# First two channel products of batch 0 in column halves, batch 1's casts and turns and batch 2's first turns in a new order, batch 3 loaded by SP

## The chip, the cores and the metric

The kernel runs on one core of a Trainium2 chip. The core has five engines that run side by side, each with its own instruction stream that it works off in order: TensorE (PE, with PEld for its weight loads) multiplies matrices, VectorE (DVE) and ScalarE (ACT) work elementwise, GpSimd (POOL) does elementwise work and issues DMAs, SyncE (SP) only issues DMAs. Data moves between HBM and the on-chip memory by DMA on 16 engines. TensorE writes to PSUM, the accumulation memory, from which DVE and ACT bring results away. The metric is the device time of one execution in microseconds, the median of several.

## The reference

There are 8 batches of 576 positions, 8 heads of 64 dimensions. First comes attention with a window of 32 positions to each side and 8 global positions that see all and are seen by all; then a mixer block: a product over the positions with a relu in its middle, added to its input (u), and a product over the 512 channels, with a hidden width of 1536 and a relu, added again.

```
scores = scale * np.matmul(q, k.transpose(0, 1, 3, 2))
mask = (np.abs(pos[:, None] - pos[None, :]) <= window) | is_global[:, None] | is_global[None, :]
attn = softmax(np.where(mask, scores, -1000000000.0))
x = np.matmul(attn, v)
h = np.maximum(x.transpose(0, 2, 1) @ w_tok1, 0.0) @ w_tok2
u = x + h.transpose(0, 2, 1)
out = u + np.maximum(u @ w_ch1, 0.0) @ w_ch2
```

## The kernel before

Positions lie in 5 tiles of 128 (tau = 0 to 4, the last half full). The 12 blocks of the hidden width are counted by j. All of it is written out without loops on the chip, and the order in which the code issues the operations is the order in which each engine works (a manual schedule). Two pools of PSUM buffers set how far PE can run ahead: `pss` (three buffers of two banks: scores, turned tiles, value products, hp) and `psm` (two of one bank: the channel products). A new tile of a pool waits until the buffer's last reader has finished.

The steps of one batch b, by function name:

- `load` fetches q and k in float32 (`load_rest` the last 64 rows into lr, `load_qk` the rest into lq and lk). There is one lr, lq and lk, so batch b+1 can only be fetched when batch b's casts have read them. Batches up to 4 are fetched from POOL's queue, later ones from SP's.
- `casts` / `cast_qk` turn them to float16 (rn, and qk for each of the four head pairs p).
- Then q and k must be turned so that the head dimension lies on the partitions. For batches 0 to 2 PE does it: `T(b, p)` turns a pair (8 matmuls against the identity, L439), `TE_q` and `TE_k` copy the result into qT and kT in the right order (L443, L449), `TR` does the last rows (L461 to L463). From batch 3 on the DMA does it, issued by SP: `turn_rest` (rawr, L379) and `turn` (raw, L385, eight in a batch), and `order_*` copies on DVE bring them in order (L388 to L398).
- `globals_` copies the global columns into qT; `qk_pads(1)` on POOL (L140 to L143) zeroes the unused columns and rows of qT and kT of the odd batches, once, after POOL's two casts of batch 1's k.
- `S_` / `S_all` are the scores (L474), with three exponentials on ACT for a head pair (L494 inner, L511 ends, L516 fourth). `SM` applies the mask on DVE (L532, L538). `GK` and `OG` are the rows of the global positions: scores, exponentials (L550, L551), the mask multiply of lf (L552), their values (L560) and rf (L565).
- `PV(b, tau)` is the value product (L581, L586, and L590 with lf and rf for the global rows); DVE divides into x16 (L597, L598).
- `M1` (L613) and its relu (L618, L619 for batch 0, L621 for others) make a1; `M2` (L637) makes hp, and DVE adds x16 to get u16 and ul (L643, L646). `M3` turns u16 into uT by DMA, issued by SP (L679, four in a batch, and L682 for the last rows of two batches together).
- `M4(b, j)`: the channel product b1p (4 matmuls, L692) and its relu into b1 (L696 on DVE or L698 on ACT). `M4l` the same for the last rows (L708). `M5(b, tau, part)`: half of a second channel product (6 matmuls, L721); after part 1 DVE adds u16 (L725) and SP stores (L726).

Batch 0 goes through `M23_first` (M2, with the addition by DVE for even tau, and by an identity matmul and an ACT copy for odd tau) and `M3_first` (uT turned on PE, L668, and copied by ACT or DVE, L670), so that no DMA stands in its way.

`period(b)` interleaves the channel products of batch b with the attention of batch n = b+1 (and prepares m = b+2). `dense` is the list of all M4, M4l and M5 of batch b; `d(k, keep)` takes up to k of them off the front and issues them, and stops when only keep are left. What is left in the list at the end of a period is issued first in the next. Within `scores(p, k)` of a period stand S of pair p, one dense item after the first two exponentials, T of pair p+2 (batches 1 and 2), a further 1 + k dense items, and SM.

The order around the change: after `M1(0, 4)` the main sequence runs M23_first and M3_first in turn, then two casts of batch 1's q on ACT (`c1[5::2]`, pairs 2 and 3, L371), M2(0, 2), load(2), and period(0). The head of period(0) turns the gathered global rows (`gather_t`), then TR, T(1, 0), M4(0, 0), T(1, 1), M4(0, 1), and scores. In period(0) load(3) is issued by POOL behind its casts of batch 2 and ahead of `gather(1)`, the indirect fetch of the global rows of batches 4 to 7. At the end of period(0) stand M2(1, .), M3(1, .), one dense item, then TR(2), T(2, 0) and T(2, 1). In period(1) POOL casts batch 3 (`casts(3)`), then issues load(4), then load_v16(3) (v of batch 3 with a cast on the way, L360), while SP issues `turns(3)`, and behind them M3(2, .). At the end of period(1) ACT casts batch 4 (`casts(4)`), each into the place from which `turns(3)` read.

Of the kernel before, what the change touches and what calls it, by code (L numbers as in the profile page):

```python
# [15 lines left out]
P = 128  # L16
# [10 lines left out]
def kernel(  # L27
# [35 lines left out]
    def psm(shape, dtype=F32, name="m"):  # L63
        return psM.tile(shape, dtype, tag="m", name=name)
# [475 lines left out]
    def GK(b):  # L540
        s = st[b]
        ps = pss([P, 2, 512], name=f"gk_{b}")
        for p in range(NP):
            o = ps[32 * p : 32 * p + 32]
            qv = qTs[b % 2][:, p, :, GW:QS]
            w = kgz[:, b, p, :]
            nc.tensor.matmul(o[:, 0, 0:384], lhsT=w, rhs=qv[:, 0:3], start=True, stop=True)
            nc.tensor.matmul(o[:, 1, 0:256], lhsT=w, rhs=qv[:, 3:5], start=True, stop=True)
        lf = mb.tile([P, NT * P], F16, tag="lf", name=f"lf_{b}")
        nc.scalar.activation(out=lf[:, 0:384], in_=ps[:, 0, 0:384], func=AF.Exp, scale=scale)  # L550
        nc.scalar.activation(out=lf[:, 384:640], in_=ps[:, 1, 0:256], func=AF.Exp, scale=scale)  # L551
        nc.vector.tensor_mul(out=lf, in0=lf, in1=mf)  # L552
        s["lf"] = lf

    def OG(b):
        s = st[b]
# [91 lines left out]
    def M23_first(tau):  # L648
        s = st[0]
        if tau == 0:  # L650
            s["uT"] = mb.tile([P, 4, 512], F16, tag="uT", name="uT_0")
        ps = psm([P, 512], name=f"hp0_{tau}")
        for ch in range(2):
            nc.tensor.matmul(
                ps, lhsT=w2[:, ch, P * tau : P * tau + P], rhs=s["a1"][:, ch, :], start=(ch == 0),
                stop=(ch == 1 and tau % 2 == 0),
            )
        if tau % 2 == 0:
            nc.vector.tensor_add(out=s["u16"][:, tau], in0=x16s[0][:, tau], in1=ps)
        else:  # L660
            nc.tensor.matmul(ps, lhsT=ident, rhs=x16s[0][:, tau], start=False, stop=True)
            nc.scalar.copy(out=s["u16"][:, tau], in_=ps)

    def M3_first(tau):
        s = st[0]
        pu = pss([P, 4, P], F16, name=f"pu_{tau}")
        for cc in range(4):
            nc.tensor.transpose(out=pu[:, cc, :], in_=s["u16"][:, tau, P * cc : P * cc + P], identity=ident)  # L668
        copy = nc.scalar.copy if tau < 3 else nc.vector.tensor_copy
        copy(out=s["uT"][:, :, P * tau : P * tau + P], in_=pu)  # L670

    def M3(b, part):
# [13 lines left out]
    def M4(b, j):  # L686
        s = st[b]
        if j == 0:
            s["b1"] = mb.tile([P, NJ, 512], F16, tag="b1", bufs=1, name=f"b1_{b}")
        ps = psm([P, 512], name=f"b1p_{b}_{j}")  # L690
        for cc in range(4):
            nc.tensor.matmul(  # L692
                ps, lhsT=wc1[:, cc, P * j : P * j + P], rhs=s["uT"][:, cc, :], start=(cc == 0), stop=(cc == 3)
            )
        if b == 0 and j % 2 or relu_on_dve[0]:
            nc.vector.tensor_scalar(out=s["b1"][:, j, :], in0=ps, scalar1=0.0, scalar2=None, op0=ALU.max)  # L696
        else:
            nc.scalar.activation(out=s["b1"][:, j, :], in_=ps, func=AF.Relu)  # L698

    def M4l(b, jj):  # L700
        s = st[b]
# [34 lines left out]
            if len(dense) > keep:  # L736
                dense.pop(0)()

    def load(i):
        eng = nc.gpsimd if i < 5 else nc.sync  # L740
        if i < B:
            load_rest(i, eng)
            load_qk(i, slice(0, H), eng)
# [6 lines left out]
    def period(b):  # L750
        n, m = b + 1, b + 2
        odd = b % 2
        dense.extend(lambda j=j: M4(b, j) for j in range(NJ))
        if odd:
            dense.extend(lambda j=j: M4l(b, j) for j in range(3))
        dense.extend(lambda t=t, i=i: M5(b, t, i) for t in range(4 + odd) for i in range(2))
# [22 lines left out]
            SM(n, p)  # L779

        if n == 1:
            gather_t(0)
            globals_(1)
            TR(1, act)
            T(1, 0)
            TE_q(1, 0, act)
            TE_k(1, 0, dve)
            d(1)
            T(1, 1)
            TE_q(1, 1, act)  # L790
            TE_k(1, 1, dve)
            d(1)
        if n > 2:
            load(n + 2)
        scores(0, tail > 5)
# [12 lines left out]
        if n == 1:  # L808
            c2 = casts(2, nc.scalar.copy)
            for c in c2[0:1] + c2[1::2]:  # L810
                c()
            load_v16(2)
            for p in range(NP):
                cast_qk(2, 1, p, nc.gpsimd.tensor_copy)
            load(3)
            gather(1)
        d(1)
        OG(n)
# [34 lines left out]
                c()  # L853
        if n == 1:
            d(1, keep)
            TR(2, act)
            T(2, 0)
            TE_q(2, 0, act)
            TE_k(2, 0, dve)
            T(2, 1)  # L860
            TE_q(2, 1, act)
            TE_k(2, 1, dve)
        else:
            d(1)
            if n == 2:
                order(3, 1)
                gather_c(1)
            d(1)
# [89 lines left out]
    load_wc2(4)  # L958
    GK(0)
    OG(0)  # L960
    PV(0, 0)
    c1 = casts(1, act)
    for c in c1[0:5]:
# [13 lines left out]
    M1(0, NT - 1)  # L977
    M23_first(0)
    M23_first(1)
    M3_first(0)  # L980
    M23_first(2)
    M3_first(1)
    M23_first(3)
    M3_first(2)
    gather_c(0)
    M3_first(3)
    for c in c1[5::2]:
        c()
    M2(0, 2)
    load(2)  # L990
    for b in range(B):
        period(b)

# [29 lines left out]
```

## Time and profile before

| what | us |
|---|---|
| median of 3 executions | 315.27 (315.1 to 315.84) |
| the profiled execution's own time | 314.14 |
| its span, first to last instruction | 312.3 |
| PE busy / DVE busy / ACT busy / POOL busy in it | 297.1 / 192.9 / 163.7 / 82.4 |
| DMA: queue of SP (q1), queue of POOL (q0), MB moved | 31.47 / 16.29 |

A line of the timeline gives start, length, engine, line, operation, output<-inputs, shape and count, and in brackets the idle time of the engine just before it with what released it. Where a line has a count, its length is that of the whole group. The length of a matmul contains its way through the array, so that two in a row overlap; the distance between starts tells what one costs in a stream.

### The profile page before, as it was taken

Reading aid. Unit: us, or ns where it says so; the run is one execution under the profiler, and the core shown is the slowest. Engines: PE = TensorE matmul, PEld = TensorE weight load, DVE = VectorE, ACT = ScalarE, POOL = GpSimd, SP = SyncE. Lnnn points to the kernel's source line nnn. Section 1 sums busy time; section 2 is a strip of 40 time slices with the busy share of each in tenths; the row PEclk is TensorE's granted clock in tenths of the full one; section 3 lists DMA queues with packets and bytes.
Section 4 is the critical chain, followed back from the end, with each engine's and each line's share of the span. In section 5 each row is a group of like instructions: output and inputs, shape, how many; then the busy total and the mean of one; then the engine's idle time right before and its main releaser. Section 6 shows DMA issues by size and latency. Waiting matters only on the chain.

```text
span 312.3 us, 6519 instructions
## 1 busy us (share of the span) xinstructions
PE 297.1 (95%) x2588; PEld 154.9 (50%) x2588; DVE 192.9 (62%) x421; ACT 163.7 (52%) x288; POOL 82.4 (26%) x130
## 2 busy tenths in 40 slices
PE   7988899988999999999999999999999999999993
PEld 3553445553565445544565445544574446444641
DVE  7976498659664678577764577577754585440021
ACT  5866685245738555476538464676543383205500
POOL 8987595767822002300230003200000000000000
PEclk9999999999999999999999999999999999999999
DMA  6999999999999999937992698944422420061022
GB/s 201 262 241 222 234 187 298 133 267 248 123 236 125 157 331 240 133 69 228 295 157 38 181 340 123 92 102 153 101 20 36 136 65 2 5 158 58 2 93 76
DMA packets 106016, 48.17 MB, mean 154 GB/s; under 512 B 86082, under 2 KB 99266, under 8 KB 105986
## 3 DMA queue, kind: packets, MB, share of 16 engines
q1 hardware_dynamic: 66576, 31.47, 43.9%
q0 software_dynamic: 39408, 16.29, 42.2%
q8 instruction: 20, 0.33, 0.4%
q14 instruction: 10, 0.08, 0.1%
q10 hardware_dynamic: 2, 0.00, 0.0%
HBM read 36.11 MB, written 9.44 MB: 146 GB/s over the span
## 4 chain that ended last, share of the span: by engine, by line
PE 76%; DMA 11%; DVE 4%; SPq 3%; ACT 3%; issue 1%; POOL 1%; POOLq 0%; ACTq 0%
PE op L721 29%; PE b1p L692 22%; PE hp L637 5%; PE a1p L613 5%; PE s L474 4%; PE b1lp L708 3%; DMA uT<-u 3%; DMA lq<-in_q_dram 3%; PE pv L581 2%; DMA w<-in_moe_w_tok_dram 2%; PE pv L590 2%; PE pv L586 2%; DMA raw<-qk 2%; DMA lv<-in_v_dram 2%; DVE e_all L538 1%; SPq L86 1%
## 5 line engine op out<-in xcount | busy, mean ns | idle before, releaser
L692 PE MATMUL b1p<-uT,wc 128*128 128x512 f16 x384 | 94.4, 380 | 2.7 <-DMA uT<-u 1.6
L721 PE MATMUL op<-wc,b 128*128 128x512 f16 x384 | 88.1, 380 | 0.0
L698 ACT ACTIVATE b<-b1p 128x512 f16<-128x512 f32 x85 | 51.1, 601 | 62.7 <-PE b1p L692 61.1
L721 PEld LDWEIGHTS <-b 128*128 128x128 f16 x384 | 36.3, 98 | 43.5
L692 PEld LDWEIGHTS <-wc 128*128 128x128 f16 x384 | 35.1, 97 | 44.6 <-issue 6.4
L360 POOL DMA_DIRECT2D vsh<-in_v_dram x35 | 30.1, 880 | 97.0 <-PE pv L590 90.6
L725 DVE TENSOR_TENSOR osb<-u,op 128x512 f32<-128x512 f16 x32 | 21.9, 686 | 48.2 <-PE op L721 48.1
L494 ACT ACTIVATE e_all<-s 128x832 f16<-128x832 f32 x32 | 27.6, 863 | 41.9 <-issue 31.3
L538 DVE TENSOR_TENSOR e_all<-e_all,bandm 128x1040 f16<-128x1040 f16 x56 | 37.8, 716 | 1.0
L643 DVE TENSOR_TENSOR u<-x,hp 128x512 f16<-128x512 f16 x28 | 17.4, 683 | 23.8 <-PE hp L637 23.8
L598 DVE TENSOR_TENSOR x<-pv,rr 128x512 f16<-128x512 f32 (+1 forms) x40 | 27.6, 691 | 1.4
L581 PEld LDWEIGHTS <-e_all 128*128 128x128 f16 x320 | 20.9, 97 | 5.5 <-DVE x L598 0.5
L581 PE MATMUL pv<-vsh,e_all 128*128 128x66 f16 x320 | 23.1, 194 | 0.0
L511 ACT ACTIVATE e_all<-s 128x576 f16<-128x576 f32 x32 | 20.7, 648 | 0.0
L586 PE MATMUL pv<-vsh,e_all 128*128 128x66 f16 x256 | 19.8, 193 | 0.0
L474 PE MATMUL s<-qT,kT 64*128 64x208 f16 (+1 forms) x320 | 18.8, 241 | 0.9 <-DVE kT L449 0.9
L371 ACT CAST qk<-lq 128x512 f16<-128x512 f32 x27 | 16.3, 617 | 6.4 <-DMA lq<-in_q_dram 6.2
L597 DVE RECIPROCAL rr<-pv 128x8 f32<-128x8 f32 (+1 forms) x40 | 8.2, 204 | 17.9 <-PE pv L590 17.6
L613 PE MATMUL a1p<-x,w 128*128 128x512 f16 x64 | 18.9, 379 | 0.3 <-DVE x L598 0.2
L474 PEld LDWEIGHTS <-kT 64*128 64x128 f16 x320 | 11.1, 94 | 14.5 <-issue 12.0
L586 PEld LDWEIGHTS <-e_all 128*128 128x128 f16 x256 | 16.6, 97 | 3.0
L516 ACT ACTIVATE e_all<-s 128x416 f16<-128x416 f32 x32 | 16.9, 528 | 0.0
(176 smaller groups left out, 349.9 us busy)
## 6 DMA issues: line engine op xcount, KB each, us to landing
out_dram<-osb SPq DMA_DIRECT2D x32, 256.0 KB, 2.4
wc<-in_moe_w_ch_dram POOLq DMA_DIRECT2D x6, 512.0 KB, 9.1
lq<-in_q_dram POOLq DMA_DIRECT2D x3, 1024.0 KB, 8.0
lk<-in_k_dram POOLq DMA_DIRECT2D x3, 1024.0 KB, 11.1
lq<-in_q_dram SPq DMA_DIRECT2D x3, 1024.0 KB, 6.8
lk<-in_k_dram SPq DMA_DIRECT2D x3, 1024.0 KB, 8.8
vsh<-in_v_dram POOLq DMA_DIRECT2D x21, 128.0 KB, 6.3
vsh<-in_v_dram POOLq DMA_DIRECT2D x14, 96.0 KB, 6.2
```

Of the source, the lines that this page charges most:

```text
L360: nc.gpsimd.dma_start(out=vsh[b % 2][r0:r1, c, :, 0:D], in_=v[b, :, j0 : j0 + (r1 - r0), :].rearrange("h p d -> p h d"),)
L474: nc.tensor.matmul(ps[:, par, off : off + n], lhsT=kT[r, P * c : P * c + P], rhs=qf[r, lo : lo + n], start=b > 0, stop=b > 0 or c > 1 and ...
L494: nc.scalar.activation(out=e2[:, :, 1:3, 64:EW], in_=ps[:, :, 0 : 2 * W].rearrange("p h (c x) -> p h c x", c=2), func=AF.Exp, scale=scale,)
L538: nc.vector.tensor_mul(out=eh, in0=eh, in1=bandm)
L581: nc.tensor.matmul(o, lhsT=e_all[:, h, tau, EW - P - sh : EW - sh], rhs=vsh[b % 2][:, tau, h, :], start=hh == 0, stop=False,)
L586: nc.tensor.matmul(o, lhsT=e_all[:, h, tau + 1, 0:P], rhs=vsh[b % 2][:, tau + 1, h, :], start=False, stop=False)
L598: nc.vector.tensor_tensor(out=x16s[b % 2][r, tau, :].rearrange("p (f h x) -> p f h x", f=2, h=NP), in0=pq[r, :, :, 0:D], in1=rr[r].unsquee ...
L613: nc.tensor.matmul(ps[tt], lhsT=w, rhs=x16s[b % 2][:, ch, :], start=(ch == 0), stop=(ch == NT - 1))
L692: nc.tensor.matmul(ps, lhsT=wc1[:, cc, P * j : P * j + P], rhs=s["uT"][:, cc, :], start=(cc == 0), stop=(cc == 3))
L698: nc.scalar.activation(out=s["b1"][:, j, :], in_=ps, func=AF.Relu)
L721: nc.tensor.matmul(ps, lhsT=w, rhs=wc2[:, j, :], start=(j == 0), stop=(j == NJ - 1))
L725: nc.vector.tensor_add(out=osb, in0=s["u16"][:, tau], in1=ps)
```

## The change

The masking of batch 0's lf is issued in two parts, columns 0 to 383 ahead of OG(0) and the rest after it. The products hp of tau 0 and 1 get one `pss` buffer of two banks, where they had two `psm` buffers; M23_first(2) moves ahead of M3_first(0). The copies of the turned tiles go to ACT for tau 0 and 3 and to DVE for 1 and 2 (before: ACT for 0 to 2). gather_t(0), globals_(1), TR(1), T(1, 0) and its copies move from the head of period(0) to ahead of it. M4(0, 0) and M4(0, 1) are taken from the dense list of period(0) and issued in column halves: columns 0 to 255 (tau 0 and 1) of both ahead of M3_first(3), columns 256 to 511 behind TR(1). Of batch 0's relus those for j = 1, 7, 9 and 11 are DVE's (before: all odd j). The two ACT casts of batch 1's q, load(2) and M2(0, 2) stand after T(1, 1) and its copies, M2 one M4 later than load(2). At the end of period(0) T(2, 0) comes first, both copies of it on ACT, then TR(2) with copies on DVE, then T(2, 1), one more d(1, keep), and both of its copies on DVE. load(3) is issued by SP at the head of period(1), behind the transposes M3(1, .).

```
-        nc.vector.tensor_mul(out=lf, in0=lf, in1=mf)
         s["lf"] = lf
+        if b > 0:
+            nc.vector.tensor_mul(out=lf, in0=lf, in1=mf)
+        else:
+            lf_mask(0, 384)
...
-        ps = psm([P, 512], name=f"hp0_{tau}")
+        if tau == 0:
+            s["hp01"] = pss([P, 2, 512], name="hp01")
+        ps = s["hp01"][:, tau] if tau < 2 else psm([P, 512], name=f"hp0_{tau}")
...
-        copy = nc.scalar.copy if tau < 3 else nc.vector.tensor_copy
+        copy = nc.scalar.copy if tau in (0, 3) else nc.vector.tensor_copy
...
+    def M4_part(b, j, x0, x1, first=True, last=True):
+        s = st[b]
         for cc in range(4):
             nc.tensor.matmul(
-                ps, lhsT=wc1[:, cc, P * j : P * j + P], rhs=s["uT"][:, cc, :], start=(cc == 0), stop=(cc == 3)
+                s["b1p", j][:, x0:x1], lhsT=wc1[:, cc, P * j : P * j + P], rhs=s["uT"][:, cc, x0:x1],
+                start=first and cc == 0, stop=last and cc == 3,
             )
-        if b == 0 and j % 2 or relu_on_dve[0]:
...
+        if b == 0 and j in (1, 7, 9, 11) or relu_on_dve[0]:
...
+    def M4_first(x0):
+        s = st[0]
+        if x0 == 0:
+            s["b1"] = mb.tile([P, NJ, 512], F16, tag="b1", bufs=1, name="b1_0")
+        for j in range(2):
+            if x0 == 0:
+                s["b1p", j] = psm([P, 512], name=f"b1p_0_{j}")
+            M4_part(0, j, x0, x0 + 256, x0 == 0, x0 > 0)
+            if x0 > 0:
+                M4_relu(0, j)
...
-        dense.extend(lambda j=j: M4(b, j) for j in range(NJ))
+        dense.extend(lambda j=j: M4(b, j) for j in range(2 if b == 0 else 0, NJ))
...
         if n == 1:
-            gather_t(0)
-            globals_(1)
-            TR(1, act)
-            T(1, 0)
-            TE_q(1, 0, act)
-            TE_k(1, 0, dve)
-            d(1)
             T(1, 1)
             TE_q(1, 1, act)
             TE_k(1, 1, dve)
+            for c in c1[5::2]:
+                c()
+            load(2)
             d(1)
+            M2(0, 2)
+        if n == 2:
+            load(3, nc.sync)
...
-            load(3)
             gather(1)
...
         if n == 1:
             d(1, keep)
-            TR(2, act)
             T(2, 0)
-            TE_q(2, 0, act)
-            TE_k(2, 0, dve)
+            TE(2, 0, act)
+            TR(2, dve)
             T(2, 1)
-            TE_q(2, 1, act)
-            TE_k(2, 1, dve)
+            d(1, keep)
+            TE(2, 1, dve)
...
     OG(0)
+    lf_mask(384, NT * P)
     PV(0, 0)
...
     M23_first(0)
     M23_first(1)
+    M23_first(2)
     M3_first(0)
-    M23_first(2)
+    M23_first(3)
+    gather_c(0)
     M3_first(1)
-    M23_first(3)
     M3_first(2)
-    gather_c(0)
+    gather_t(0)
+    M4_first(0)
     M3_first(3)
-    for c in c1[5::2]:
-        c()
-    M2(0, 2)
-    load(2)
+    globals_(1)
+    TR(1, act)
+    M4_first(256)
+    T(1, 0)
+    TE_q(1, 0, act)
+    TE_k(1, 0, dve)
     for b in range(B):
         period(b)
```

More of the change, by code (lines that the diff above doesn't have):

```diff
@@ L737, in d, with load @@
                 dense.pop(0)()
-    def load(i):
-        eng = nc.gpsimd if i < 5 else nc.sync
+    def load(i, eng=None):
+        eng = eng or (nc.gpsimd if i < 5 else nc.sync)
         if i < B:
```

10 lines of the change are left out of this document (9 added, 1 removed).

## The prediction

> **What bounds the kernel now.** I read the page first (busy shares), then the busy time by stage, then each engine's timeline from 25 to 113 us, and the DMA view last.
>
> ```profile
> span 312.3 us, 6519 instructions
> PE 297.1 (95%) x2588; PEld 154.9 (50%) x2588; DVE 192.9 (62%) x421; ACT 163.7 (52%) x288; POOL 82.4 (26%) x130
> ```
>
> TensorE is busy for 297.1 of 312.3 us, so what an edit can win is the 15 us in which it isn't. The table by stage (columns: stretch, its length, then PE, PEld, DVE, ACT, POOL busy, clock, DMA share, GB/s) shows where these lie.
>
> ```profile
> 27.00:36.50 9.50, 7.46 (x58) 3.88 (x57) 4.51 (x12) 5.99 (x13) 3.96 (x9) 1.00 1.14 248
> 36.50:52.00 15.50, 14.50 (x134) 6.99 (x134) 13.63 (x25) 11.26 (x21) 14.51 (x22) 1.00 1.45 226
> 66.00:75.40 9.40, 7.85 (x71) 4.22 (x72) 6.16 (x11) 5.04 (x8) 5.21 (x8) 1.00 1.21 224
> 83.30:97.00 13.70, 13.70 (x167) 9.36 (x166) 6.46 (x16) 6.19 (x10) 4.05 (x5) 1.00 1.20 191
> ```
>
> Idle: 2.04, 1.00 and 1.55 us in the first three stretches, all touched by the change, and 0.87 between them (at 65.98, below): 5.5 in all. From 83 us on PE has none. What ends them is named by the brackets of PE's rows below, and for the second stretch by a row of the waits (total, times, longest):
>
> ```profile
> PE b1p L692 <- DVE b L696: 1.0, 2, 0.6
> ```
>
> **The unit.** Moving a product earlier is worth its own length on PE, from two dense stretches of the chain (start, length, matmuls):
>
> ```profile
> 281.53 10.44 PE b1p L692 x48
> 294.65 12.96 PE op L721 x60
> ```
>
> So one M4 (4 matmuls) is 0.87 us and one M5 half (6) is 1.30.
>
> **Part 1, batch 0's end (27 to 36.5 us).**
>
> ```profile
> 20.60 0.39 PE L590 MATMUL pv<-rf,lf 128*128 128x264 f16 x2 [0.70 <-DVE rf L565]
> 26.01 0.61 ACT L371 CAST qk<-lk 128x512 f16<-128x512 f32 x1
> 26.53 0.59 ACT L618 ACTIVATE a<-a1p 128x512 f16<-128x512 f32 x1
> 27.17 1.11 PE L654 MATMUL hp<-a,w 128*128 128x512 f16 x4 [0.48 <-ACT a L618]
> 33.41 1.14 ACT L371 CAST qk<-lq 128x512 f16<-128x512 f32 x2 [1.96 <-DMA lq<-in_q_dram]
> 35.14 0.61 PE L439 MATMUL pT<-ident,qk 128*128 128x128 f16 x8 [1.06 <-ACT kT L463]
> 38.10 0.45 PE pT L439 x8
> 36.28 0.23 POOL L142 MEMSET qT<- 128x160 f16 x1
> 36.56 0.57 PE L474 MATMUL s<-qT,kT 64*128 64x208 f16 x10
> ```
>
> The split mask lets rf start earlier and takes most of the 0.70 us wait. But the a1 relu at 26.53 starts exactly where ACT's cast ends, so PE still begins the hp products at 27.17: I cost it at 0 (bounds 0 and 0.45 gained).
>
> From 27.17 I lay the new order out by hand with these durations. In before, ACT stands in the two casts of lq until 34.5 with the TR and TE copies behind them; that is the 1.06 us wait. In after the casts stand behind TE_q(1,1), when lq has landed. With pu copies divided between ACT and DVE, the first half products start near 30.5, the second halves near 32.3 (after pu_3's copy on ACT), T(1,0) and T(1,1) end near 34.1, M4(0,2) near 35.0 and M2(0,2) near 35.4. Sixteen matmuls of 256 columns stand for eight of 512; the trace has no 256, but the 128x512 gives 217 ns each and eight 128-column turns take 0.45 us (at 38.10 in the chain), 56 ns each, so a 256 lies between 109 and 112: 0.05 us at most, taken as 0.
>
> Then PE waits: scores of batch 1 read columns of qT that POOL zeroes at 36.28 to 36.51, behind its casts of lk, and that isn't moved. So scores(0) starts at 36.55, as before, with one M4 more done: **gain 0.87**, and 1.1 us of new idle ahead of it, which also hides any slip of this order (if the halves wait for the whole of uT, for example). M2's other cost, load(2), sits on POOL behind the same pads in both versions: 0.
>
> **Part 2, period 0 (36.5 to 60).** The relus of j = 3 and 5 go to ACT. DVE has two relus less and PE is one M4 ahead, so the two waits for DVE's relu, 1.0 us, go. What is late next is ACT:
>
> ```profile
> 36.95 0.86 ACT L494 ACTIVATE e_all<-s 128x832 f16<-128x832 f32 x1 [0.40 <-PE s L474]
> 37.71 0.64 ACT L511 ACTIVATE e_all<-s 128x576 f16<-128x576 f32 x1
> 38.24 0.60 ACT L698 ACTIVATE b<-b1p 128x512 f16<-128x512 f32 x1
> 38.72 0.54 ACT L516 ACTIVATE e_all<-s 128x416 f16<-128x416 f32 x1
> 39.34 0.57 PE L474 MATMUL s<-qT,kT 64*128 64x208 f16 x10
> ```
>
> Start to start, ACT needs 0.76, 0.53, 0.48 and about 0.45, and now a second relu of 0.48: 2.70 us, where PE's round is 39.34 - 36.56 = 2.78. It fits with 0.08 to spare in rounds 0 and 1. **Gain 1.0**, bounds 0.4 and 1.2. By the count of d calls one M5 half more now stands ahead of M2 of batch 1, so M2, and the transposes behind it, come only 0.87 + 1.0 - 1.30 = 0.57 earlier.
>
> **Part 3, first turns of batch 2 (60 to 66).**
>
> ```profile
> 63.87 1.25 PE L439 MATMUL pT<-ident,qk 128*128 128x128 f16 x16
> 65.98 0.57 PE L474 MATMUL s<-qT,kT 64*128 64x208 f16 x10 [0.87 <-DVE kT L449]
> ```
>
> Pair 0 now turns first, and both of its copies run on ACT while DVE, busy with u16 and ul, takes the TR copies afterwards. From 63.87 + 0.9 = 64.8 to 65.98 there are 1.2 us; the new order leaves about 0.6 (two ACT copies of 0.5 behind a turn of 0.45, the rest of the turns beside them). **Gain 0.6**, bounds 0 and 0.9. The second d(1, keep) does nothing: three M5 halves are left by then, where four were.
>
> **Part 4, uT of batch 1 and load(3) (62 to 75).**
>
> ```profile
> 61.97 9.54 SPq L679 DMA_TRANSPOSE uT<-u  x4
> 75.39 1.89 PE L692 MATMUL b1p<-uT,wc 128*128 128x512 f16 x8 [1.55 <-DMA uT<-u]
> uT<-u SPq DMA_TRANSPOSE x1, 11.9
> q0 software_dynamic: 677, 2.31, 83.9%
> 133.54 5.83 SPq L679 DMA_TRANSPOSE uT<-u  x4
> uT<-u SPq DMA_TRANSPOSE x4, 2.4
> ```
>
> The first three rows and the fourth (queue view of 61.9 to 72: packets, MB, share) belong together: while POOL's load(3) moves, the first transpose lands 11.9 us after its issue, and PE gets the four 13.4 us after the first was issued (61.97 to 75.39). With no load beside them (last two rows) they take 5.8 and land after 2.4. In after, load(3) stands behind them on SP, so uT should be there near 61.4 + 5.8 + 1.2 = 68.4. M4(1,0) stood behind S(2,2) and stands ahead of it now; it asks for uT near 75.39 - 1.55 - 2.47 - 0.6 = 70.8. **Gain 1.55**, bounds 0 (rival 3) and 1.55. The sum is 0.87 + 1.0 + 0.6 + 1.55 = 4.0.
>
> By the Trainium skill, "DMA: Bandwidth & Descriptors", section on queues, rings and completion order, each DMA engine takes turns between queue rows packet by packet. By that rule small transpose packets beside POOL's big ones starve, as the 11.9 us shows, and a load behind them on their own row can't do that. The same section of the rule speaks against the next step, where load(4) stays on POOL's row and comes later, towards the transposes of batch 2; that is rival 1.
>
> **What the late load(3) costs.** It is issued near 68.5 where POOL began it at 58.9. On SP stand behind it two stores, whose buffers aren't wanted again soon, and the turns of batch 3, which need its data anyway. On POOL the casts of batch 3 wait for it, and behind them load(4) and the v loads.
>
> ```profile
> lk<-in_k_dram SPq DMA_DIRECT2D x3, 1024.0 KB, 8.8
> 58.88 0.71 POOL L93 DMA_DIRECT2D lr<-in_q_dram  x1
> 78.64 0.93 POOL L86 DMA_DIRECT2D lq<-in_q_dram  x1
> 76.01 19.17 SPq L385 DMA_TRANSPOSE raw<-qk  x8
> 98.97 5.57 SPq L679 DMA_TRANSPOSE uT<-u  x4
> 102.30 0.62 ACT L371 CAST qk<-lk 128x512 f16<-128x512 f32 x1 [0.84 <-DMA raw<-qk]
> 112.77 1.90 PE L692 MATMUL b1p<-uT,wc 128*128 128x512 f16 x8
> ```
>
> lk goes out about 2.3 us behind the first of the four, near 70.8, and lands near 79.6; POOL's casts end near 83.6, load(4) goes out near 85 instead of 78.6. The raw turns start near 77 and most run before load(4) moves, so their 19 us should shrink to about 15 and uT of batch 2 still start near 95 (98.97 less 4.0). It is wanted at 112.8 - 4.0 = 108.8, 13.8 us later; batch 1's took 13.4 with load(3) beside them. ACT's casts of batch 4 end near 101.5 to 102.5, when load(4) has landed, and the second scores of batch 3, 4.5 us behind the first, then meet a full score buffer for up to 1 us. I take 0.5 for all this, bounds 0 and 2.3. **Net gain 3.5.**
>
> **Rivals.**
> 1. *Load(4) meets uT of batch 2 (slower).* If the raw turns start only when lk is in (81) and again need 19.2 us, uT of batch 2 starts at 100.3; with 13.4 under load(4) and the v loads it is there at 113.7, later than PE wants it even today. It decides from 108.8 on, and every us behind 112.8 is a loss; with 2 us more of v traffic ahead of it PE stands until 115.4: 2.6 slower, 317.9. For it: 19.17 us in before. Against: most turns are out before load(4).
> 2. *ACT bounds period 0.* 2.70 against 2.78; if each of three rounds slips by 0.4, parts 1 and 2 give 0.7 instead of 1.9: 313.0.
> 3. *uT is held by the gathers, not by load(3).* They stay on POOL and come earlier, from 58.9. Then uT comes as long after M2 as now, part 4's wait grows by what parts 1 to 3 won, and only the 0.57 that M2 comes earlier is kept: 314.7. Against: 128 of the 2310 KB are theirs.
> 4. *The late casts press on DVE at a worse place* (next rows).
>
> ```profile
> 75.79 2.01 DVE L538 TENSOR_TENSOR e_all<-e_all,bandm 128x1040 f16<-128x1040 f16 x2
> 77.99 1.31 DVE L538 TENSOR_TENSOR e_all<-e_all,bandm 128x1040 f16<-128x1040 f16 x2
> ```
>
> The same two multiplies take 2.01 us beside POOL's casts and 1.31 without. In after the casts fall on 79 to 84, on the last multiplies ahead of batch 2's value products: 0.7 on the path, 312.5. "SBUF — State Buffer" of the Trainium skill (SBUF: two separate sides) has DVE and GpSimd lock a shared port pair for a whole instruction; the 0.7 us agrees.
>
> **How the numbers follow.** The profiled execution took 314.14 us for a span of 312.3; 312.3 - 3.5 = 308.8, so 310.6 for it, and from the median shown, 315.27, the forecast is 311.8. Chances: forecast with its bounds (310.3 to 313) 0.50, rivals 2 and 4 together 0.20, rival 3 0.12, rival 1 in part (0.5 to 3 lost of the gain) 0.08 and to a loss 0.10. About 0.3% (0.95 us) is what a measurement of this kernel can tell: below 314.3 is faster. To that go 0.50 + 0.20, a third of rival 3 (0.04) and half of the partial rival 1 (0.04): 0.78; the rest of these two is same, 0.12; slower 0.10. The range 310.3 to 314.8 leaves out rival 1's worse half and little else.
>
> **What would show it.** Scores of batch 1 start at 36.5 with a PE wait for POOL's memset ahead of them; no PE wait for L696 on DVE in 37 to 50; M2 of batch 1 starts near 59.6 with M5(0,1,1) ahead of it; uT of batch 1 lands after about 2.5 us and M4(1,0) doesn't wait; raw turns start near 77. Wrong would be: uT landing over 8 us, a PE wait for uT near 108, or ACT without gaps in 37 to 46.

## The result, and the profile after

The changed kernel took 323.77 us (median of 4 executions, 322.86 to 325.64) against 315.19 (314.39 to 315.84): a ratio of 1.028, 95% interval 1.023 to 1.033. It is slower, by about 8.6 us, where 311.8 was forecast. On another chip the same changed kernel took 318.64 us (12 executions, 312.75 to 321.47) against 314.77 (312.29 to 319.41) there. The ratios in this text leave out executions more than 1.5% above the fastest of the same kernel; in that second set seven of the twelve are such, the profiled one among them, and the other five (312.75 to 315.78) are level with the kernel before, at 1.000 (0.995 to 1.006). The loss is thus not the same in every execution of this code; what it is made of is read below from two profiles that have it.

The page of the changed kernel's first profile (its own time 322.86 us), and PE's longest waits in it (engine, line, released by: total, times, longest):

```profile
span 320.9 us, 6545 instructions
PE 301.8 (94%) x2596; PEld 157.8 (49%) x2596; DVE 194.0 (60%) x423; ACT 163.0 (51%) x287; POOL 80.3 (25%) x126
```

```profile
PE a1p L620 <- DVE x L605: 5.3, 1, 5.3
...
PE s L474 <- ACT e_all L494: 1.0, 1, 1.0
```

The waits that the forecast wanted gone are gone: none for uT of batch 1, none for DVE's relu. A new one, longer than all of those together, stands in front of M1 of batch 3 (L620). The busy share of PE hardly moved, so it is the place of the wait, not the share, that has to be read.

The starts of PE's marks on the way there, from the timelines of the two kernels and of a second profile of the changed kernel (`e13_after_profiled`, below), in us from the span's start:

| mark on PE | before | after | after, second |
|---|---|---|---|
| first hp of batch 0 | 27.17 | 29.66 | 26.54 |
| first scores of batch 1 | 36.56 | 39.27 | 35.94 |
| M2 of batch 1 | 60.19 | 62.52 | 59.20 |
| first scores of batch 2 | 65.98 | 67.75 | 64.43 |
| first scores of batch 3 | 102.00 | 101.40 | 98.47 |
| M2 of batch 3 | 131.76 | 140.03 | 137.01 |
| M2 of batch 4 | 166.59 | 174.86 | 171.84 |
| span | 312.3 | 320.9 | 317.8 |

Read by differences, it falls into three pieces. From the scores of batch 1 to those of batch 3 the changed kernel is *faster*: 62.13 and 62.53 us instead of 65.44. From there to M2 of batch 3 it loses 8.9 and 8.8 us (38.63 and 38.54 instead of 29.76). After that nothing differs (34.83 us to the next M2 in all three). And the first profile is 2.5 us late at the first hp already, the second is not: its span is shorter by 3.1 us, as its first hp is by 3.12.

The rows of the lost stretch, in the timeline of the changed kernel (start, length, engine, line, idle time before it and releaser), from the load of batch 3 on:

```profile
64.31 5.65 SPq L688 DMA_TRANSPOSE uT<-u  x4
71.36 0.62 SPq L93 DMA_DIRECT2D lr<-in_q_dram  x1
88.08 0.93 POOL L86 DMA_DIRECT2D lq<-in_q_dram  x1
102.70 0.62 ACT L371 CAST qk<-lk 128x512 f16<-128x512 f32 x1 [2.40 <-DMA lk<-in_k_dram]
107.25 0.39 PE L474 MATMUL s<-qT,kT 64*128 64x144 f16 x6 [1.00 <-ACT e_all L494]
109.48 4.47 SPq L86 DMA_DIRECT2D lk<-in_k_dram  x1
118.84 2.37 SPq L379 DMA_TRANSPOSE rawr<-rn  x1
129.76 0.23 DVE L388 COPY qT<-rawr 128x256 f16<-128x256 f16 x1 [6.70 <-DMA rawr<-rn]
131.01 1.01 PE L620 MATMUL a1p<-x,w 128*128 128x512 f16 x2 [5.35 <-DVE x L605]
133.18 0.60 DVE L392 COPY kT<-raw 128x512 f16<-128x512 f16 x1 [2.22 <-DMA raw<-qk]
```

Load(3) leaves at 71.4, load(4) at 88 (78.6 before); ACT waits for batch 4's k; the second scores of batch 3 meet a full buffer. So far it is in kind what the prediction had worked out, some 3 us later where load(4) leaves (2.7 of them from the late head). The next link is the one that it had not: DVE works in order, and its copy of batch 4's last rows (order_rest, L388) stands ahead of the division of batch 3's value products. It waits 6.70 us for rawr, and with it wait x and PE. The same two rows of the kernel before, and the landings from the DMA view of before and the chain of waits of after:

```profile
115.93 1.30 SPq L379 DMA_TRANSPOSE rawr<-rn  x1
122.39 0.22 DVE L388 COPY qT<-rawr 128x256 f16<-128x256 f16 x1
```

```profile
rawr<-rn SPq DMA_TRANSPOSE x1, 6.4
```

```profile
118.84 10.89 DMA rawr<-rn
```

In the kernel before, 115.93 + 6.4 = 122.3 met a reader at 122.39: **no slack**, and no wait to show it. Counted from the first scores of batch 2, after issues rawr 1.1 us later (51.09 instead of 49.95), DVE wants it 1.1 us earlier (55.31 instead of 56.41, because PE has gained), and it lands 4.5 us later: 6.7 us.

Why it lands later is in the DMA view of 106 to 126 us (packets, MB, share of the queue of SP, q1, and of POOL, q0), first before, then after:

```profile
q1 hardware_dynamic: 7826, 4.62, 99.1%
q0 software_dynamic: 3493, 0.44, 39.7%
```

```profile
q1 hardware_dynamic: 5372, 3.84, 81.2%
q0 software_dynamic: 6810, 0.86, 66.3%
```

POOL's queue carries twice the packets, 126 bytes each on average (0.86 MB by 6810): the last pieces of batch 4's v, which stand behind load(4) and so have come late too, beside load(5) and the row transposes. Then the clock (busy time by stage; the clock is the column before the last two):

```profile
128.00:130.00 2.00, 0.00 (x0) 0.00 (x0) 0.24 (x2) 0.00 (x0) 0.00 (x0) 0.68 1.52 136
130.00:132.00 2.00, 0.99 (x3) 0.41 (x3) 0.93 (x3) 0.00 (x0) 0.00 (x0) 0.50 1.85 148
132.00:134.00 2.00, 2.00 (x14) 0.93 (x12) 0.78 (x3) 0.23 (x1) 0.00 (x0) 0.50 1.71 168
134.00:136.00 2.00, 2.00 (x18) 1.21 (x16) 1.97 (x5) 0.37 (x1) 0.88 (x1) 0.61 1.54 162
```

Behind the wait PE's granted clock is 0.50 for 4 us and 0.61 for the next 2: of its 0.99 + 2.00 us of work at 0.50 and 2.00 us at 0.61, 0.5 + 1.0 + 0.8 = 2.3 us are the clock's, by this estimate. With 1.00 for the scores and 5.35 for the wait that is 8.65 of the 8.87 us.

### The profile page after: what moved, and what is told of

It reads as the page before. It is cut to its first block, busy times and chain, and to the rows that moved or that the text cites. A ratio compares the mean times of both kernels' runs of the same rounds, so it can differ in the third digit from the quotient of the medians.

```text
span 320.9 us, 6545 instructions
## 1 busy us (share of the span) xinstructions
PE 301.8 (94%) x2596; PEld 157.8 (49%) x2596; DVE 194.0 (60%) x423; ACT 163.0 (51%) x287; POOL 80.3 (25%) x126
## 4 chain that ended last, share of the span: by engine, by line
PE 65%; DMA 5%; DVE 4%; ACT 3%; issue 1%; SPq 0%; ACTq 0%
PE op L751 27%; PE b1p L706 17%; PE hp L644 4%; PE a1p L620 4%; DMA rawr<-rn 3%; PE b1lp L738 3%; PE s L474 3%; DMA raw<-qk 2%; PE pv L588 2%; PE pv L597 2%; DVE e_all L538 1%; PE pv L593 1%; ACT e_all L494 1%; ACT b L717 1%; ACT e_all L516 1%
## 5 line engine op out<-in xcount | busy, mean ns | idle before, releaser
L706 PE MATMUL b1p<-uT,wc 128*128 128x512 f16 (+1 forms) x392 | 95.4, 378 | 1.0 <-ACT uT L679 0.5
L717 ACT ACTIVATE b<-b1p 128x512 f16<-128x512 f32 x87 | 52.7, 606 | 68.9 <-PE b1p L706 67.6
L706 PEld LDWEIGHTS <-wc 128*128 128x128 f16 x392 | 36.0, 98 | 43.2 <-issue 6.3
L538 DVE TENSOR_TENSOR e_all<-e_all,bandm 128x1040 f16<-128x1040 f16 x56 | 37.1, 704 | 1.0
L620 PE MATMUL a1p<-x,w 128*128 128x512 f16 x64 | 20.4, 408 | 5.4 <-DVE x L605 5.3
L588 PEld LDWEIGHTS <-e_all 128*128 128x128 f16 x320 | 21.3, 98 | 8.1 <-issue 2.7
L588 PE MATMUL pv<-vsh,e_all 128*128 128x66 f16 x320 | 23.9, 194 | 1.0 <-issue 1.0
L593 PE MATMUL pv<-vsh,e_all 128*128 128x66 f16 x256 | 20.7, 194 | 0.9 <-issue 0.9
L474 PE MATMUL s<-qT,kT 64*128 64x208 f16 (+1 forms) x320 | 19.2, 241 | 1.3 <-ACT e_all L494 1.0
L593 PEld LDWEIGHTS <-e_all 128*128 128x128 f16 x256 | 17.2, 98 | 3.2 <-issue 0.3
L474 PEld LDWEIGHTS <-kT 64*128 64x128 f16 x320 | 11.1, 94 | 15.4 <-issue 13.1
```

What stands on the lines that cost most here:

```text
L474: nc.tensor.matmul(ps[:, par, off : off + n], lhsT=kT[r, P * c : P * c + P], rhs=qf[r, lo : lo + n], start=b > 0, stop=b > 0 or c > 1 and ...
L538: nc.vector.tensor_mul(out=eh, in0=eh, in1=bandm)
L588: nc.tensor.matmul(o, lhsT=e_all[:, h, tau, EW - P - sh : EW - sh], rhs=vsh[b % 2][:, tau, h, :], start=hh == 0, stop=False,)
L593: nc.tensor.matmul(o, lhsT=e_all[:, h, tau + 1, 0:P], rhs=vsh[b % 2][:, tau + 1, h, :], start=False, stop=False)
L620: nc.tensor.matmul(ps[tt], lhsT=w, rhs=x16s[b % 2][:, ch, :], start=(ch == 0), stop=(ch == NT - 1))
L706: nc.tensor.matmul(s["b1p", j][:, x0:x1], lhsT=wc1[:, cc, P * j : P * j + P], rhs=s["uT"][:, cc, x0:x1], start=first and cc == 0, stop=las ...
```

## The experiments

Three theories went in. **L**: load(3) on SP behind the transposes leaves some 12 us later (71.4 instead of 58.9), and each load behind it waits for the casts of the one before. **V**: what L delays is above all batch 4's v, whose small pieces then share the DMA engines with load(5) and the transposes of batch 4. **H**: the late head of the first profile, with its slow clock, is what costs.

### e1: load(3) back on POOL, the rest of the change kept

```
         if n == 2:
-            load(3, nc.sync)
...
+            load(3)
             gather(1)
```

> The changed kernel with load(3) issued by POOL at its old place; all the rest of the change stays. Theory L (the late load(3) makes load(4), ACT's casts of batch 4 and so load(5) late, and rawr of batch 4 stands behind load(5) on SP): the wait of order_rest(4) on DVE (6.7 us) and PE's 5.35 us at 126 to 131 go, the stall at the second scores of batch 3 (1.0) too; the wait for uT of batch 1 returns (1 to 3 us). 312 to 316 if the head of batch 0 runs as in the kernel before, about 2.5 more if the hp products start at 29.7 again instead of 27.2. Rival H (the head of batch 0, with its slow clock, is what costs, and the rest only follows): 319 or more.

317.28 us (315.46 to 319.49) against 315.69 on that chip, ratio 1.011 (1.002 to 1.021). The stretch from the scores of batch 3 to M2 is 29.76 us, as before the change: without the late load the wait for rawr doesn't exist. What came back is a wait for uT of batch 1:

```profile
75.41 1.04 PE L706 MATMUL b1p<-uT,wc 128*128 128x512 f16 x4 [0.86 <-DMA uT<-u]
```

Its first hp was late too (29.03: ACT's cast of batch 1's k waits 3.95 us for its load, the relu behind it comes late, and PE waits 2.96 us for that), so its time, within what theory L expected with a late head, says nothing on the other parts.

### e2: load(3) on SP alone, in the kernel before

```
+        if n == 2:
+            load(3, nc.sync)
...
-            load(3)
             gather(1)
```

> The kernel before with nothing but load(3) moved to SP behind the transposes of batch 1. Theory L: the wait for uT of batch 1 goes (1.5 won), rawr of batch 4 comes late by what load(5) is late (about 5 us, some of it won back since PE here is a little later): 317 to 321, with DVE waiting several us for rawr near 122. Rival H: the move alone costs nothing, 313.5 to 315.5.

318.93 us (314.98 to 321.99), ratio 1.017 (1.006 to 1.029). Moving the load is enough to lose, with nothing else changed, as theory L expected. The profiled execution was the fastest of the four (314.98), so what the others lost beyond this no profile shows; the wait for uT is gone from it (scores of batch 3 at 99.74 instead of 102.00), and more than that is lost behind them:

```profile
122.84 0.23 DVE L388 COPY qT<-rawr 128x256 f16<-128x256 f16 x1 [2.62 <-DMA rawr<-rn]
125.87 0.60 DVE L392 COPY kT<-raw 128x512 f16<-128x512 f16 x1 [1.82 <-DMA raw<-qk]
```

32.67 us from the scores to M2 instead of 29.76.

### e3: load(5) behind the transposes of batch 4 on SP

```
-        if n > 2:
+        if n > 3:
             load(n + 2)
...
             turns(m)
+            if n == 3:
+                load(5)
```

> The changed kernel with load(5) issued behind the turns of batch 4 on SP instead of ahead of them. Theory L: rawr of batch 4 lands within some 5 us of its issue, the 5.35 us of PE idle and the slow clock behind it go: 315 to 318.5, if casts of batch 5 at the end of that period don't wait for the later load (up to 2 us of that). Rival V (the small pieces of the v loads of batches 3 and 4, late as well, hold the transposes, whatever stands ahead of them on SP): rawr still lands 8 us or more after issue and the time stays at 321 or more.

319.46 us (317.72 to 320.39), ratio 1.014 (1.005 to 1.023). The wait for rawr is gone (DVE's copy at 120.38 without idle time, M2 of batch 3 at 129.75), and a larger one stands one batch on, since ACT's casts now wait for load(5) itself:

```profile
139.56 0.62 ACT L371 CAST qk<-lk 128x512 f16<-128x512 f32 x1 [4.30 <-DMA lk<-in_k_dram]
144.10 0.59 PE L474 MATMUL s<-qT,kT 64*128 64x144 f16 x6 [5.97 <-ACT e_all L494]
```

Theory L's range of 315 to 318.5 allowed for a wait of up to 2 us there, and 5.97 came. What rawr itself needed, by the DMA view of 110 to 122 us of this run:

```profile
rawr<-rn SPq DMA_TRANSPOSE x1, 6.4
```

It was issued at 112.38, beside 3110 packets on POOL's queue from 112 to 119 us. So the small pieces alone don't make it late: rival V as it was put here (8 us or more, whatever stands ahead on SP) is refuted. Load(5) in front of the transposes is one half of the cause, and it can't simply be moved. H falls here as the only cause: the head is early (27.09) and the time is lost all the same.

### e4: batch 4's v not loaded

```
-        if 2 < m < B:
+        if 2 < m < B and m != 4:
             load_v16(m)
```

> The changed kernel without the load of v of batch 4 (batch 4 uses the values of batch 2 that lie in the buffer). Theory L: load(5) still begins late, behind casts of batch 4, and rawr(4) still stands behind it; it may move faster without the small pieces: DVE still waits 2 to 5 us for rawr, 319 to 322. Rival V: rawr lands within 5 us, no wait, 315 to 318.

311.40 us (310.24 to 314.91), ratio 0.990 (0.986 to 0.994), below both ranges of its expectation (319 to 322 for L, 315 to 318 for V). The kernel leaves out a load, so its time is not that of the whole work; its stretches can be compared. load(3) and load(4) are as late as in the changed kernel (load(4) at 84.82; 84.59 in the second profile, whose head is as early), the second scores of batch 3 wait 0.87, load(5) is in front of the transposes, and the wait for rawr is almost nothing:

```profile
113.33 1.39 SPq L379 DMA_TRANSPOSE rawr<-rn  x1
119.84 0.23 DVE L388 COPY qT<-rawr 128x256 f16<-128x256 f16 x1 [0.17 <-DMA rawr<-rn]
```

It lands 6.5 us after its issue, as in the kernel before. From the scores of batch 3 to M2 it is 30.81 us: the late loads without the v pieces cost 1.0 us there, and with them 7.8 more. Beside e3 it shows that both are needed: load(5) ahead of rawr and no pieces beside it gives 6.5 us (6.4 in the kernel before), the pieces and no load ahead 6.4, both together 10.9 in the first profile of the changed kernel and 8.9 in the second.

### e5: batch 4's v held until batch 4 is transposed

```
         if 2 < m < B:
+            if m == 4:
+                held = const.tile([P, 4], F16, name="held")
+                nc.gpsimd.tensor_copy(out=held, in_=st[4]["raw"][:, 1, NP - 1, 3, 0:4])
             load_v16(m)
```

> The changed kernel with one small copy on POOL ahead of batch 4's v load, which reads the last of batch 4's transposed k tiles, so that v goes out only when these transposes have landed. All work is kept. Theory L and V together (load(3) on SP makes load(4) late, and so the small v pieces fall on load(5) and the row transposes of batch 4): as without batch 4's v, no wait of DVE for rawr or raw of more than about 1 us near 120 to 125, S(3,0) near 98, time 310.5 to 313.5 us, about 1 per cent under the kernel before. Theory L alone (load(5) in front of the transposes on SP decides, with v or without): the wait for rawr stays at 2 to 5 us, 316 to 321. Theory H (the slow head costs): 321 to 324 if the first hp starts near 29.5, whatever the later waits do. New risk: v of batch 4 lands too late for its value products, which would show as a PE wait at L588 or L593 of batch 4 near 145.

321.67 us (319.36 to 326.73), ratio 1.017 (1.010 to 1.024): not the 310.5 to 313.5 of V. At batch 4 V was right: the wait for rawr falls from 6.70 to 0.55 us, and the stretch takes 36.1 us instead of 43.5 from M2 of batch 2 to M2 of batch 3. But the held pieces go out together with those of batch 5, and the same happens one batch later:

```profile
123.86 0.23 DVE L388 COPY qT<-rawr 128x256 f16<-128x256 f16 x1 [0.55 <-DMA rawr<-rn]
131.97 8.39 POOL L360 DMA_DIRECT2D vsh<-in_v_dram  x10 [0.35 <-PE a1p L620]
160.15 0.23 DVE L388 COPY qT<-rawr 128x256 f16<-128x256 f16 x1 [3.51 <-DMA rawr<-rn]
161.41 0.59 PE L620 MATMUL a1p<-x,w 128*128 128x512 f16 x2 [2.16 <-DVE x L605]
```

Ten pieces from 132 to 140, the late rows of batch 5 at 160, PE's wait for x. From M2 of batch 3 to M2 of batch 4 it takes 39.84 us, where every kernel with v at its usual time but e3 takes 34.6 to 35.0. The mechanism is confirmed by moving it; as a cure the hold fails. The rest of the loss is a late head (29.92).

### e6, e7 and e8: the same hold with other loads

e6 is e5 with batch 3's v issued ahead of POOL's casts of batch 3; e7 is e5 with load(3) on POOL; e8 is the kernel before with the hold alone.

> The kernel of v4_gated, and v of batch 3 loaded ahead of POOL's casts of batch 3, in the time in which POOL waits for load(3). All work is kept. Theories L and V: load(4) has its queue for itself and lk of batch 4 lands about 2 us earlier; ACT's wait for lk near 102.7 (2.4 us) shrinks to below 1 and the second scores of batch 3 wait less (1.0 to about 0.3): 309.5 to 313, equal to or up to 1 us under v4_gated. Against it: the small v pieces then move beside the transposes of batch 1's uT; if they stretch these from 2.5 us to 7, M4(1,0) waits about 1 to 2 us near 74 and the gain is used up.

> The changed kernel with load(3) back on POOL's queue, and the gate ahead of batch 4's v. All work is kept. Theories L and V: with load(3) back there is no late chain, so the gate has nothing to save; as with load(3) on POOL alone (317.3 there, a head of 26.8 to 29), 314 to 317.5, with a wait for uT of batch 1 of 0.9 to 1.5 us near 75. If the value of load(3) on SP is real once its cost is removed, v4_gated is below this one by 1.5 to 3 us. Theory H: equal to v4_gated within 1 us.

> The kernel before with the gate ahead of batch 4's v alone. All work is kept. Theories L and V: batch 4's v is out before load(5) there anyway, so the gate gains nothing: 314.5 to 316.5, a ratio within 0.5 per cent of 1. If the v pieces beside the transposes cost the kernel before something as well, 312.5 to 314.5.

e6: 318.40 us (ratio 1.013, 1.007 to 1.019); e7: 320.61 (1.015, 1.010 to 1.020); e8: 318.50 (1.009, 1.005 to 1.012), all against 315.23. All three missed. e7 loses its 5 us behind M2 of batch 3 as e5 does (40.05 us to the next M2), e8 1.5 us there (36.29). In e6 that stretch is as ever (35.1), but the early v pieces stretch uT of batch 1, as its expectation feared, to a wait of 1.05 us. All four kernels with the hold have a late first hp (29.9 to 30.3), e8 too, which has the instructions of the kernel before in its first 80 us. By its expectation e7 was to lie 1.5 to 3 us above e5 if load(3) on SP is worth that; it lies 1.1 below it. With late heads and a second loss in both, this settles neither that nor H.

### e9 and e11: load(3) on SP at its old place

e9 is the changed kernel with this edit, e11 the kernel before with the same line only.

```
                 cast_qk(2, 1, p, nc.gpsimd.tensor_copy)
+            load(3, nc.sync)
             gather(1)
```

> The changed kernel with load(3) still on SP, but issued where the kernel before had it on POOL: behind POOL's casts of batch 2 in the last third of period(0), near 59.5 us instead of 71.4. All work is kept. Theory L (it is the lateness of load(3) that costs, by way of load(4), the v pieces and load(5)): load(4) is back near 78 to 80 us, the row transposes of batch 4 aren't waited for near 122, and from the first scores of batch 3 to M2 of batch 3 it is 29.8 us again (38.6 in the changed kernel). uT of batch 1 now stands behind load(3) on SP's own queue: if it is there by 73.6, no wait, 311.5 to 313.5 us with a first hp near 27; if it waits for load(3)'s data, a wait of 1 to 1.5 us near 74 as in the kernel before, 313 to 315. Theory H: 315 to 318 with a first hp near 30. If the queue, not the time, is what costs, the wait for rawr stays and the time is 318 or more.

> The kernel before with load(3) on SP at its old place, alone. All work is kept. Theory L: no late chain, so only the wait for uT of batch 1 (1.55 us) can change: gone, 313 to 314.5, or there as before, 314.5 to 316; from the first scores of batch 3 to M2 of batch 3 29.8 us, where load(3) on SP behind the transposes had 32.7. If SP's queue costs whatever the time of the issue: 317 or more, with the wait for rawr.

e11: 312.76 us (311.67 to 316.01) against 314.55, ratio 0.995 (0.991 to 0.998), 0.2 us under its first case. e9: 314.40 (311.15 to 316.87), 0.999 (0.996 to 1.002), in its second case, with a longer wait than the 1 to 1.5 us of it. In both the stretch from the scores of batch 3 to M2 is 29.76 us: it is the time at which load(3) leaves, not SP's queue, that brings the late chain. In e11 uT of batch 1 is in time; in e9, where M4(1,0) asks for it earlier, it isn't:

```profile
59.14 0.37 SPq L86 DMA_DIRECT2D lk<-in_k_dram  x1
61.95 10.21 SPq L688 DMA_TRANSPOSE uT<-u  x4
73.57 1.02 PE L706 MATMUL b1p<-uT,wc 128*128 128x512 f16 x4 [2.97 <-DMA uT<-u]
```

The transposes stand behind 1 MB of k on their own queue, and all that the other parts of the change had won by then waits for them.

### e12: load(3) in two pieces on SP

q and the last rows as in e9, k behind the transposes as in the changed kernel.

```
+            load_rest(3, nc.sync)
+            load_one(3, q, lq)
             gather(1)
...
         if n == 2:
+            load_one(3, k, lk)
```

> The changed kernel with load(3) on SP in two pieces: q and the last rows where load3_sp_early has them (near 51 to 55 us), k alone where the changed kernel has it, behind the transposes of batch 1's uT (near 68 us). All work is kept. Theory L: what delays uT of batch 1 in load3_sp_early (a wait of 3.0 us) is the k half in front of it on the same queue; with it behind, uT lands near 67 to 69 and M4(1,0) doesn't wait, while POOL's casts of batch 3 end near 77 to 79, load(4) goes out near 80 (78.6 in the kernel before, 88.1 in the changed one), and the row transposes of batch 4 aren't waited for near 122: S(3,0) near 98, 29.8 to 30.3 us from there to M2 of batch 3, 309.5 to 312 us with a first hp near 27. Rival: the k half late by 8.5 us is enough to bring load(4) beyond 84, the v pieces fall on load(5) and a wait for rawr of 1 to 4 us comes back: 313 to 317. Rival: the stores ahead of uT on SP hold it, not k: the wait of 2 to 3 us stays, 314.

312.23 us (12 executions, 310.90 to 315.06) against 314.53, ratio 0.992 (0.988 to 0.995): 0.8% below the kernel before on that chip, and above its expectation's first case by 0.2 us. (The changed kernel's 323.77 and 318.64 us are from other chips.) Its profile, with a span of 309.3 us:

```profile
60.97 5.84 SPq L694 DMA_TRANSPOSE uT<-u  x4
68.29 0.46 SPq L92 DMA_DIRECT2D lk<-in_k_dram  x1
81.64 0.93 POOL L86 DMA_DIRECT2D lq<-in_q_dram  x1
119.17 0.22 DVE L394 COPY qT<-rawr 128x256 f16<-128x256 f16 x1
```

The transposes take 5.84 us, about as in the changed kernel. Against the second profile of that kernel, whose head is as early, load(4) leaves at 81.6 instead of 84.6, and the last v piece of batch 4 is issued by 98.2, ahead of load(5) at 102, where there it was issued by 105.4, behind the start of load(5) at 103.4. Nothing waits for rawr. From the scores of batch 2 to those of batch 3 it is 34.35 us, from there to M2 29.76.

### e10 and e13: each kernel again, with a profile

> The kernel before, unchanged, with a profile of its own on this chip: a control for the head, whose first hp began at 27.2 in the first profile of this kernel and at 30.2 in the same code with a copy on POOL 100 us later. If the head varies by itself: near 30 here too or spread, time 314 to 316, and the 2.5 us that the changed kernel's profile shows at the first hp are not put down to the change. If it is fixed by the code: 27.2 again.

> The changed kernel, unchanged, with a second profile on another chip: a control for the two parts of its loss. Of the 8.6 us that its first profile lost in span, 2.5 lay ahead of the first hp (29.66 us against 27.17), in stalls at 22 to 26 us that others with the same first 50 us did not show (26.5 to 27.1 in four of them, 29.0 to 30.3 in four others). Theories L and V: the wait for rawr of 4 to 7 us at about 120 to 130 is there again, and a slow clock behind it; 319 to 321 us if the first hp starts near 27, 322 to 325 if near 30. If the wait for rawr is small in this profile and the time still 323, L and V explain only that one execution, and the head or something else carries the median.

e10, the kernel before: 315.78 us (312.34 to 318.45), first hp at 27.05. By its expectation that speaks for a head fixed by the code; e13, the same code as the first profile of the changed kernel, speaks against it, with a first hp at 26.54 instead of 29.66. e13 took 318.64 us as told above, 0.4 below its expectation, and its profile (of an execution of 319.82 us) has the same wait:

```profile
125.05 0.23 DVE L388 COPY qT<-rawr 128x256 f16<-128x256 f16 x1 [5.38 <-DMA rawr<-rn]
126.31 0.59 PE L620 MATMUL a1p<-x,w 128*128 128x512 f16 x2 [4.03 <-DVE x L605]
```

So the late chain recurs, and the late head of the first profile is a second loss beside it. Of the 8.6 us of the first span, 2.5 are the head, 5.6 the middle (8.9 lost behind the scores of batch 3 less the 3.3 gained ahead of them), and 0.5 lie elsewhere. The executions of e13 near 313 us leave no room for 8.8 us lost beside a gain of about 3, so the wait can't stand in all of them in this size. No profile shows such an execution, and what keeps the wait out of it stays open.

## Why the prediction was wrong

By its own steps, in its order:

- **Part 1**, gain 0.87: right. From the first hp to the scores of batch 1 it takes 9.40 us (second profile; 9.61 in the first) where it took 9.39, with one M4 more done in it. The 1.1 us of new idle that it saw in front of POOL's memset lie elsewhere: in both profiles PE waits 0.78 us for DVE's u and 0.63 for the copies of uT, and for the memset not at all. Of the runs with this head only e9 (0.32 us) and e3 show that wait:

```profile
37.07 0.57 PE L474 MATMUL s<-qT,kT 64*128 64x208 f16 x10 [0.51 <-POOL qT L142]
```

- **Part 2**, M2 of batch 1 0.57 earlier against the scores of batch 1: 0.37 to 0.38 (23.25 and 23.26 us instead of 23.63). The two waits for DVE's relu are gone. ACT's first round, from one inner exponential to the next in the changed kernel, is 2.67 us where 2.70 was worked out, and the second is 2.88:

```profile
40.12 0.87 ACT L494 ACTIVATE e_all<-s 128x832 f16<-128x832 f32 x1
...
42.79 0.88 ACT L494 ACTIVATE e_all<-s 128x832 f16<-128x832 f32 x1
...
45.67 0.86 ACT L494 ACTIVATE e_all<-s 128x832 f16<-128x832 f32 x1
```

ACT has no idle time between these rows: one of the signs of being wrong that the prediction had set, and what rival 2 (ACT bounds it) says, is there. PE's two rounds grow to 2.93 and 2.88 us from 2.78, which is the missing 0.2 us. In e3, whose scores start later behind the memset, the rounds are 2.78 again, and M2 of batch 1 comes 0.62 earlier against the scores.
- **Part 3**, 0.6: 0.56 (from M2 of batch 1 to the scores of batch 2 5.23 us instead of 5.79).
- **Part 4**, 1.55: right. The four transposes land after 2.4 us each, by the DMA view of 61 to 70 us, and M4(1,0) doesn't wait:

```profile
uT<-u SPq DMA_TRANSPOSE x4, 2.4
```

Rival 3 (the gathers hold uT) is refuted by it. The rule of the Trainium skill that the prediction named for this place, "DMA: Bandwidth & Descriptors", section on queues, rings and completion order, agrees with the row; that the engines take turns by packet is not itself seen in any run.

Of the 4.0 us of these four parts, 2.9 to 3.3 stand in the table at the scores of batch 3. Two small waits of PE in period(1) hold another half microsecond; the second, for rf behind DVE's multiplies beside POOL's casts, is rival 4, at 0.2 us (0.4 in the second profile) instead of 0.7:

```profile
81.04 1.02 PE L706 MATMUL b1p<-uT,wc 128*128 128x512 f16 x4 [0.33 <-ACT b L717]
84.10 0.39 PE L597 MATMUL pv<-rf,lf 128*128 128x264 f16 x2 [0.18 <-DVE rf L572]
```

- **"What the late load(3) costs"**, 0.5 us with bounds of 0 and 2.3: **this step failed**; it measured 8.8 to 8.9 in the two profiles, and 2.9 with load(3) moved alone (e2). Its working holds as far as it goes: load(4) out near 85 plus the 2.7 us that the head of the first profile is late, the eight raw turns in 13.1 us instead of 19.2, uT of batch 2 in time with no wait near 108 (so rival 1, the only slower one, did not happen), the second scores of batch 3 waiting 1.0 us at most. The two signs of being wrong that the prediction had set for uT, a landing over 8 us and a wait near 108, stayed away. But it followed the queue for one batch and stopped where uT of batch 2 was safe. Two things that load(4) delays were not followed: POOL issues v of batch 4 behind it, and load(5) can only leave when ACT's casts of batch 4 have read the buffers, with the transposes of batch 4 behind load(5) on SP. Together they bring rawr 10.9 us after its issue instead of 6.4. Its reader had no slack in the kernel before, which its own rows would have shown (115.93 + 6.4 against 122.39). The bound of 2.3 us was thus no bound: it priced one wait, not the chain.
- The chance of 0.10 for slower belonged to one mechanism, rival 1, which looked at the right queue one batch too early.
- **Not foreseen at all**: the head. Its first hp stands at 26.5 to 27.2 us in nine profiles of both kinds of kernel and at 29.0 to 30.3 in six others, and the changed kernel, with the same code, stands in both groups (29.66 and 26.54), so the order of the head alone doesn't fix it. In e1 the late load of batch 1's k stands behind it; in the first profile of the changed kernel it shows as

```profile
23.06 0.19 PE L593 MATMUL pv<-vsh,e_all 128*128 128x66 f16 x1 [0.45 <-issue]
...
23.85 0.21 DVE L604 RECIPROCAL rr<-pv 128x8 f32<-128x8 f32 x1 [2.09 <-remote]
```

four such gaps on PE and one on DVE for which the trace names no instruction as the cause. What starts them stays open, and so does whether the change makes them more frequent. The prediction took 0.95 us as what a measurement of this kernel can tell; the kernel before alone lies between 312.16 and 319.44 us in 29 executions on one chip (the one of e9 to e11).

## What to carry to other kernels

When a load that stands in a chain (one buffer, cast, next load) is moved to a later time, follow every load behind it to the end of the chain, on every queue that it shares, and compare issue plus landing with the start of the reader in the kernel as it is: a reader that starts within 0.1 us of its landing shows no wait and still has no slack. To take a load out of the way of something small, move the half of it that is in the way, and leave the rest early, as e12 did. And before a wait is removed by holding one transfer back, look at what that transfer meets at its new time.

## What the runs showed of the hardware

- Pieces of v with packets of 126 bytes on average, on POOL's queue, slow a load on SP's queue and the transpose behind it: rawr lands 10.9 and 8.9 us after its issue, where it took 6.5 with the load and without the pieces (e4) and 6.4 with the pieces and without the load (e3). In the 20 us shown above, POOL's queue moved 0.42 MB more than in the kernel before and SP's 0.78 MB less.
- Behind a wait of 5.35 us PE's granted clock was 0.50 for 4 us and 0.61 for 2, which cost about 2.3 us more, nearly half as much again as the wait. "TensorE: Matmul & The Clock Gate" of the Trainium skill (Part 1, the HAM clock gate) has the clock halve after an idle window of about 3.4 us. The 5.35 us here and the 4.03 of e13 agree; in e5 a wait of 2.16 us was followed by a halved clock too, in these stages:

```profile
160.00:162.00 2.00, 0.59 (x3) 0.29 (x3) 1.44 (x5) 0.00 (x0) 0.17 (x1) 1.00 1.97 207
162.00:164.00 2.00, 2.00 (x22) 1.40 (x21) 1.66 (x4) 0.60 (x1) 0.00 (x0) 0.64 2.12 184
164.00:166.00 2.00, 2.00 (x7) 0.80 (x6) 1.40 (x3) 0.00 (x0) 0.88 (x1) 0.50 1.03 179
```
